# Attention and MLP block on one core: scores in bfloat16, and one exponential for some pairs of tiles

## The chip, the core and the metric

The kernel runs on one core of a Trainium2 chip. Its engines work side by side, each through its own queue in order: TensorE (PE in the profile, PEld for its weight loads), VectorE (DVE), ScalarE (ACT), GpSimd (POOL) and SyncE (SP), which here only issues DMAs. Engines wait for each other through semaphores. The metric is the device time in microseconds (us) of one execution; lower is better.

## The reference

A transformer block over 2048 tokens of width 640 with a modulation computed from a vector `c`. First attention with 32 heads of 128 against caches of 2048 keys and values, then a token-mixing MLP. The part that matters here is the attention:

```python
sa, ca, ga, sb, cb, gb = ...            # six rows from silu(c) @ w_mod
h = _layernorm(x) * (1 + ca) + sa
q = (h @ wq).reshape(B, Sq, H, Dh).transpose(0, 2, 1, 3)
scores = einsum('bhqd,bhkd->bhqk', q, k_cache) * Dh ** (-0.5)
p = softmax(scores)
o = einsum('bhqk,bhkd->bhqd', p, v_cache)
x = x + ga * (o.transpose(...).reshape(B, Sq, H * Dh) @ wo)
h = _layernorm(x) * (1 + cb) + sb
x = x + gb * B(h)                       # layernorm, w1, gelu, shifts, w2, then w3, gelu, w4
```

All inputs and the output are bfloat16.

## The kernel before

Work is written as a list of operations for each engine (class `Prog`); each names the keys it reads and writes, and the class derives the semaphore waits. An engine carries out its operations in the order in which they were written. An operation that reads what an earlier one of the same engine wrote waits for that one too, on DVE, ACT and GpSimd.

The attention stage is one loop over `s` (line 553), 512 tiles of 128 queries: head `h = s // 16`, tile `j = s % 16`. Step `s` does the following.

- PE computes the scores of the tile, 128x2048, into the PSUM tensor `Sps` in two halves of 1024 (`qk`, lines 301 and 15). Between the halves it multiplies the probabilities of the tile eight steps back, `g_ = s - PVD` with `PVD = 8`, by V (`pv`, line 314, 16 matrix products into `PTp`), and does pieces of other work: a query projection for the next head (`q_piece`, line 246), or a transposition on PE (`t_piece`, line 262).
- DVE reads each half of the scores from PSUM, multiplies by minus the scale, writes the result as fp32 to a ring of three slots, `negS[:, s % 3]`, and keeps the minimum of the half in `nm0` or `nm1` (line 594). The profile shows the write of the minimum as a separate instruction.
- GpSimd takes the smaller of the two minima (line 604), and ACT computes `exp(nm - negS)` over 128x2048 into the ring of probabilities `Pb`, ten slots (line 607). The per-partition `nm` is the bias operand.
- The probabilities have to be transposed for the product with V. For most tiles SP issues a DMA transpose, of two tiles at once where both of an even and odd pair go by DMA (`transpose`, line 231). Two tiles a head (3 and 10), three in every fourth head (2, 3 and 10), are transposed by PE instead, in two halves of 1024 columns, and each half is copied from PSUM by ACT (line 271); for tiles 2 and 3 DVE copies the second half (line 273, `by_dve`).
- On odd steps ACT copies the attention output of two tiles from PSUM to `Of` (line 585), and it copies finished query chunks to `QT` (line 253).
- Four steps later (`LAG`) GpSimd normalizes: for each group of four tiles one reciprocal of the row sums (`rcp`, line 455), a multiplication for each tile (`norm`, line 462) and, after the fourth, a store to a scratch in HBM, issued from GpSimd's own DMA queue (line 469).
- SP also issues the loads of K (line 214, a DMA transpose), wq and V for the following heads, in the same queue as the transposes.

PSUM holds only one tile of scores, so PE writes the next half as soon as DVE has read it, and PE, DVE, GpSimd, ACT, SP and DMA form a loop: the product with V for tile `s - 8` stands in PE's queue among the scores of tile `s`.

After the loop follow the output projection, the layernorms and the MLP, in which neither `Sps` scores nor exponentials occur; `negS` is reused there as storage.

Of the kernel before, what the change touches and what calls it, by code (L numbers as in the profile page):

```python
# [7 lines left out]
ACT = mybir.ActivationFunctionType  # L8
BF16 = mybir.dt.bfloat16
F32 = mybir.dt.float32  # L10
# [113 lines left out]
def bass_adaLN_cond__mha_block_cached__mixer_s_mlp__prompt_kernel(  # L124
# [3 lines left out]
    _, H, SK, DH = A_k_cache.shape  # L128
# [3 lines left out]
    NQT = SQ // 128  # L132
# [13 lines left out]
    with ExitStack() as es:  # L146
# [11 lines left out]
        if True:  # L158
            with ExitStack() as es1:
                sb1 = lambda name, shape, dt: es1.enter_context(nc.sbuf_tensor(name, shape, dt))  # L160
                RP = 10
                PVD = 8
                PE_STEPS = ({3: 6, 10: 13}, {2: 5, 3: 7, 10: 14})
                kind = lambda h: 1 if h % 4 == 1 else 0
                US = KT * (SQ + 4)
                sb1("pad", [128, 32], F32)
                ring = sb1("ring", [128, 2 * RP, SK], BF16)
                negS = sb1("negS", [128, 3, SK], F32)
                wo = sb1("wo", [128, H, D], BF16)
                kv = sb1("kv", [128, 2 * SK + 2 * NKT * 130 + 2 * KT * 128 + 2 * SQ], BF16)  # L170
                small = sb1("small", [128, 4 * NQT + 32], F32)
                hTx = sb1("hTx", [128, US], BF16)
                Of = sb1("Of", [128, 4, 2, 130], F32)
                On = sb1("On", [128, 2, 4, 128], BF16)
# [1 line left out]
                sd = small[:, 2 * NQT:3 * NQT]  # L176
                rstd = small[:, 3 * NQT:4 * NQT]
                nm0, nm1, nm, rl = [small[:, 4 * NQT + 8 * i:4 * NQT + 8 * i + 8] for i in range(4)]
                hT = hTx[:, 0:KT * SQ].rearrange("p (k q) -> p k q", k=KT)
                o1 = 2 * SK  # L180
                o2 = o1 + 2 * NKT * 130
# [5 lines left out]
                Pb = ring[:, 0:RP]  # L187
# [22 lines left out]
                G = Prog(nc, es1, "a")  # L210
# [61 lines left out]
                    else:  # L272
                        G.op("vector", lambda v: v.tensor_copy(dst, src), r=[("J", jb)], w=[("PT", g % RP, r)])  # L273

                by_dve = lambda g, r: r == 1 and g % NQT in (2, 3)
                PIECES = []
                for steps in PE_STEPS:
                    taken = [u for j in steps.values() for u in range(2 * j, 2 * j + 4)]
# [68 lines left out]
                if H > 1:  # L347
# [8 lines left out]
                     r=["id0"], w=["ident"])  # L356
# [122 lines left out]
                tmp = flat[:, 0:4 * D].bitcast(F32).rearrange("p (b d) -> p b d", b=2)  # L479
                xt = flat[:, XT0:XT0 + NQT * D].rearrange("p (t d) -> p t d", t=NQT)  # L480
                xb = flat[:, XB0:XB0 + 2 * NQT * D].bitcast(F32).rearrange("p (t d) -> p t d", t=NQT)
                negb = negS[:].rearrange("p r s -> p (r s)").bitcast(BF16)
                gT = [flat[:, GT0:GT0 + NFT4].rearrange("p (f q) -> p f q", f=NFT),
                      negb[:, 0:NFT4].rearrange("p (f q) -> p f q", f=NFT)]
                OTj = [hTx[:, 0:2 * H * 128].rearrange("p (h q) -> p h q", q=128),
# [15 lines left out]
                rst = sm[:, 288:288 + 3 * NQT].rearrange("p (l t) -> p l t", l=3)  # L501
                vet = sm[:, 336:336 + 3 * NQT].rearrange("p (l t) -> p l t", l=3)
                mhalf = sm[:, 384:385]
                NEG = [("negS", i) for i in range(3)]
                KVK = ([("KT", b) for b in range(2)] + [("V", b) for b in range(2)] + [("wq", b) for b in range(2)]
                       + [("QT", b, cc) for b in range(2) for cc in range(NQC)])
                HTK = [("hT", cc, k) for cc in range(NQC) for k in range(KT)]
# [43 lines left out]
                LAG = 4  # L551
                for s in range(NG + PVD + LAG):
                    h, j = divmod(s, NQT)
                    g_ = s - PVD
                    evacs = []
                    if s <= 2:
                        for i in ((0,), (1, 2), range(3, len(MROW)))[s]:
                            mod_rows(i)
                    if s == 3:
                        G.op("gpsimd", lambda g: g.tensor_scalar(  # L560
                            out=mod_bc[:, 2 * D:3 * D], in0=mod_bc[:, 2 * D:3 * D], scalar1=1.0, scalar2=1.0, op0=ALU.add, op1=ALU.mult),
                            r=[("mod", i) for i in range(len(MROW))], w=["mod"])
                    for half in range(2):
                        if s < NG:
                            qk(s, half)
                        if half == 0 and s in (NG + PVD - 5, NG + PVD - 4):
                            b0 = a_pe(0, None if s == NG + PVD - 5 else b0, (s - NG - PVD + 5,))
                        if half == 0 and s == NG + PVD - 2:
                            b1 = a_pe(1, None, (0,))
                        if 0 <= g_ < NG:  # L570
                            pv(g_, half)
                        if s == 0 and half == 1:
                            q_head0(NQC - 1)
                        if h + 1 < H and 2 * j + half in PIECES[kind(h)]:
# [13 lines left out]
                    for fn, x, y in evacs:  # L588
                        if fn is q_evac or not by_dve(x, y):
                            fn(x, y)  # L590
                    for half in range(2):
                        if s < NG:
                            r8 = s % 8
                            G.op("vector", lambda v, half=half, s=s, r8=r8: v.tensor_scalar(  # L594
                                out=negS[:, s % 3, half * 1024:(half + 1) * 1024],
                                in0=Sps[:, half * 1024:(half + 1) * 1024],
                                scalar1=-SCALE, scalar2=None, op0=ALU.mult, op1=ALU.min,
                                accum_out=(nm0 if half == 0 else nm1)[:, r8:r8 + 1]),
                                r=[("S", half)], w=[("negS", s % 3), ("nmh", half, r8)])
                    for fn, x, y in evacs:  # L600
                        if fn is t_evac and by_dve(x, y):
                            fn(x, y)
                    if s < NG:
                        G.op("gpsimd", lambda g, r8=r8: g.tensor_scalar(  # L604
                            out=nm[:, r8:r8 + 1], in0=nm0[:, r8:r8 + 1], scalar1=nm1[:, r8:r8 + 1], scalar2=None, op0=ALU.min),
                            r=[("nmh", 0, r8), ("nmh", 1, r8)], w=[("nm", r8)])
                        G.op("scalar", lambda a, s=s, r8=r8: a.activation(  # L607
                            Pb[:, s % RP, :], negS[:, s % 3, :], ACT.Exp, bias=nm[:, r8:r8 + 1], scale=-1.0),
                            r=[("negS", s % 3), ("nm", r8)], w=[("Pb", s % RP)])
                        if not is_pe(s):  # L610
                            if s % 2 == 1 and not is_pe(s - 1):
                                transpose(s - 1, 2)
                            elif s % 2 == 1 or is_pe(s + 1):
                                transpose(s, 1)
                        if j == 2 and h >= 1 and h + 1 < H:
                            load_k(h + 1)
                        if h + 1 == H and j in (2, PVD + 1):
                            i = 0 if j == 2 else 1
                            load_ot(0, OTC[i], OTC[i + 1], i)
                        if j == 6 and h + 2 < H:  # L620
                            load_wq(h + 2)
# [72 lines left out]
                for n in range(KT):  # L694
                    lst = []
                    p = 0
                    while p < 128:
# [8 lines left out]
                        p = pe_  # L706
# [203 lines left out]
```

## Time and profile before

| | |
|---|---|
| runs, median (3 runs) | 1574.97 us (1573.75 to 1576.16) |
| profiled execution: span from first to last instruction | 1568.9 us |
| first score instruction of DVE | 35.4 us |
| last score instruction of DVE ends | 1251.8 us |
| granted TensorE clock, mean | 0.998 |
| moved by DMA over the span | 334.59 MB |

The page gives for the profiled execution the span only; the runs' times include what lies around it. A line of the groups has the source line, the engine, the operation, what is written and read with shapes and types, the count, then the busy time in us and the mean of one in ns, and then the idle time of the engine just before them with what ended it. A line of the timeline has the start in us from the span's start, the time taken, the engine and the group; in square brackets stands the idle time before it. "SPq" is SP's queue of DMA issues. A line of waits has who waited, for whom, us in total, how many times, and the longest. The stage of interest lies between 35 and 1252 us, 32 heads one after the other.

### The profile page before, as it was taken

Reading aid. Unit: us, or ns where it says so; the run is one execution under the profiler, and the core shown is the slowest. Engines: PE = TensorE matmul, PEld = TensorE weight load, DVE = VectorE, ACT = ScalarE, POOL = GpSimd, SP = SyncE. Lnnn points to the kernel's source line nnn. Section 1 sums busy time; section 2 is a strip of 40 time slices with the busy share of each in tenths; the row PEclk is TensorE's granted clock in tenths of the full one; section 3 lists DMA queues with packets and bytes.
Section 4 is the critical chain, followed back from the end, with each engine's and each line's share of the span. In section 5 each row is a group of like instructions: output and inputs, shape, how many; then the busy total and the mean of one; then the engine's idle time right before and its main releaser. Section 6 shows DMA issues by size and latency. Waiting matters only on the chain.

```text
span 1568.9 us, 33553 instructions
## 1 busy us (share of the span) xinstructions
PE 1472.3 (94%) x13947; PEld 923.4 (59%) x13175; DVE 1398.3 (89%) x2471; ACT 1275.9 (81%) x1121; POOL 623.0 (40%) x1396
## 2 busy tenths in 40 slices
PE   5899999999999999999999999999999899999999
PEld 3466666666665566566656666566566655554545
DVE  6999999999999999999999999999999937667435
ACT  4999999999999999999999999999999900034230
POOL 0144444444444444444444444444444433323100
PEclk9999999999999999999999999999999999999999
DMA  9999999999999999999999999999999999725100
GB/s 298 239 221 239 237 242 237 233 241 243 237 240 233 239 232 232 240 236 235 229 237 236 233 243 249 226 242 243 235 241 237 238 246 190 157 53 144 38 22 34
DMA packets 1172828, 334.59 MB, mean 213 GB/s; under 512 B 1153280, under 2 KB 1166656, under 8 KB 1172672
## 3 DMA queue, kind: packets, MB, share of 16 engines
q1 hardware_dynamic: 1164192, 311.30, 100.8%
q0 software_dynamic: 6144, 16.79, 3.5%
q10 hardware_dynamic: 2336, 4.34, 0.8%
q8 instruction: 108, 1.77, 0.5%
q14 instruction: 48, 0.39, 0.1%
HBM read 43.48 MB, written 19.40 MB: 40 GB/s over the span
## 4 chain that ended last, share of the span: by engine, by line
ACT 40%; DVE 23%; PE 19%; DMA 9%; issue 7%; POOL 1%; POOLq 0%; DVEq 0%
ACT ring L607 32%; DVE negS L594 20%; DMA ring<-ring 8%; PE Sps L540 8%; PE Sps L847 4%; ACT ring L271 3%; ACT kv L253 2%; ACT Of L585 2%; PE QPp L798 2%; PE Oaug L798 2%; DVE ring L273 1%; PE Sps L783 1%; DVE ring L379 1%; DMA negS<-o_scratch 1%; PE PTp L314 1%
## 5 line engine op out<-in xcount | busy, mean ns | idle before, releaser
L594 DVE TENSOR_SCALAR_CACHE_REDUCE negS<-Sps 128x1024 f32<-128x1024 f32 x1024 | 1177.7, 1224 | 19.4 <-PE Sps L15 18.5
L607 ACT ACTIVATE ring<-negS,small 128x2048 bf16<-128x2048 f32 x512 | 1045.7, 2066 | 13.7 <-POOL small L604 12.5
L314 PEld LDWEIGHTS PTp<-kv,ring 128*128 128x128 bf16 x8192 | 554.1, 98 | 325.0 <-issue 69.6
L314 PE MATMUL PTp<-kv,ring 128*128 128x129 bf16 x8192 | 645.3, 220 | 25.0 <-DMA ring<-ring 23.9
L15 PE MATMUL Sps<-kv 128*128 128x512 bf16 x1024 | 387.9, 379 | 16.8 <-DVE negS L594 9.9
L604 POOL TENSOR_SCALAR small<-small 128x1 f32<-128x1 f32 x512 | 146.4, 286 | 621.8 <-DVE negS L594 621.7
L301 PE MATMUL Sps<-kv 128*128 128x512 bf16 x919 | 354.3, 386 | 27.8 <-DVE negS L594 16.5
L462 POOL TENSOR_SCALAR On<-Of,small 128x128 bf16<-128x128 f32 x512 | 191.0, 373 | 13.0
L301 PEld LDWEIGHTS Sps<-kv 128*128 128x128 bf16 x1024 | 98.1, 96 | 141.7 <-DVE negS L594 121.6
L455 POOL TENSOR_TENSOR small<-Of,small 128x4 f32<-128x4 f32 x128 | 133.1, 1040 | 8.8 <-ACT Of L585 8.7
L469 POOL DMA_DIRECT2D o_scratch<-On x128 | 103.1, 806 | 40.8 <-POOL On L462 37.2
L585 ACT COPY Of<-PTp 128x259 f32<-128x259 f32 x256 | 108.6, 424 | 13.2 <-PE PTp L314 13.2
L246 PE MATMUL Oaug<-hTx,kv 128*128 128x512 bf16 x268 | 101.9, 385 | 3.7 <-DVE hTx L411 3.7
L246 PE MATMUL QPp<-hTx,kv 128*128 128x512 bf16 x259 | 97.7, 382 | 2.6 <-ACT hTx L406 2.1
L728 ACT ACT_TABLE_LOAD x1 | 1.3, 1283 | 112.6 <-POOL hTx L746 112.6
L594 DVE DVE_READ_ACCUMULATOR negS<-Sps 128x1 f32 x1024 | 90.3, 88 | 0.0
L271 ACT COPY ring<-Oaug 128x1024 bf16<-128x1024 bf16 x72 | 77.0, 1069 | 0.0
L641 POOL TENSOR_SCALAR negS<-negS 128x1 f32<-128x1 f32 x48 | 24.2, 504 | 125.2 <-DVE negS L650 125.2
L540 PE MATMUL Sps<-wo,negS 128*128 128x128 bf16 (+1 forms) x503 | 69.9, 298 | 1.2 <-DMA negS<-o_scratch 0.8
L540 PE MATMUL Sps<-wo,hTx 128*128 128x512 bf16 (+1 forms) x502 | 69.3, 297 | 0.5
L851 DVE TENSOR_TENSOR ring<-Sps,ring 128x640 f32<-128x640 f32 x15 | 12.4, 824 | 59.5 <-PE Sps L847 59.5
L655 DVE TENSOR_TENSOR ring<-Sps,mod_bc 128x640 f32<-128x640 f32 x16 | 13.1, 821 | 53.6 <-PE Sps L540 32.9
(88 smaller groups left out, 1052.7 us busy)
## 6 DMA issues: line engine op xcount, KB each, us to landing
kv<-in_A_v_cache_dram SPq DMA_DIRECT2D x32, 512.0 KB, 5.0
o_scratch<-On POOLq DMA_DIRECT2D x128, 128.0 KB, 4.7
kv<-in_A_wq_dram SPq DMA_DIRECT2D x32, 160.0 KB, 3.2
wo<-in_A_wo_dram SPq DMA_DIRECT2D x1, 5120.0 KB, 16.5
ring<-ring SPq DMA_TRANSPOSE x248, 7.1
ring<-in_A_x_dram SPq DMA_DIRECT2D x5, 640.0 KB, 6.6
ring<-in_w_mod_dram SPq DMA_DIRECT2D x1, 3200.0 KB, 13.8
out_dram<-wo SPq DMA_DIRECT2D x15, 160.0 KB, 1.8
```

What stands on the lines that cost most here:

```text
L15: return t.add_instruction(mybir.InstMatmult(name=t.bass.get_next_instruction_name(), ins=[t.lower_ap(rhs), t.lower_ap(lhsT)], outs=[t.low ...
L246: G.op("tensor", lambda t: t.matmul(JB[jb], wq[:, hb, q, :], hT[:, q, cc * 512:(cc + 1) * 512], start=(q == 0), stop=(q == KT - 1)), r=[(" ...
L271: G.op("scalar", lambda a: a.copy(dst, src), r=[("J", jb)], w=[("PT", g % RP, r)])
L301: ins = (t.matmul if c2 == 0 else partial(same_weights, t))(Sps[:, col:col + 512], QT[:, hb, j * 128:(j + 1) * 128], KTs[:, hb, col:col + ...
L314: ins = t.matmul(ob[:, 0:129], PTs[:, b, kt, :], Vaug[:, hb, kt, 0:129], start=(kt == 0), stop=(kt == NKT - 1))
L455: G.op("gpsimd", lambda g: g.tensor_tensor(out=rl[:, 4 * b:4 * b + 4], in0=Of[:].rearrange("p a z d -> p (a z) d")[:, 4 * b:4 * b + 4, 128 ...
L462: G.op("gpsimd", lambda g: g.tensor_scalar(out=On[:, b, z, :], in0=Of[:, 2 * b + z // 2, z % 2, 0:128], scalar1=rl[:, 4 * b + z:4 * b + z ...
L540: ins = t.matmul(YB[b][:, c0:c0 + cw], OTj[pr % 2][:, 2 * hh + z, :], wo[:, hh, c0:c0 + cw], start=(hh == 0), stop=(hh == H - 1))
L585: G.op("scalar", lambda a, p=p: a.copy(Of[:, p % 4].rearrange("p z d -> p (z d)")[:, 0:259], PO[:, (p % 2) * 512:(p % 2) * 512 + 259]), r= ...
L594: G.op("vector", lambda v, half=half, s=s, r8=r8: v.tensor_scalar(out=negS[:, s % 3, half * 1024:(half + 1) * 1024], in0=Sps[:, half * 102 ...
L604: G.op("gpsimd", lambda g, r8=r8: g.tensor_scalar(out=nm[:, r8:r8 + 1], in0=nm0[:, r8:r8 + 1], scalar1=nm1[:, r8:r8 + 1], scalar2=None, op ...
L607: G.op("scalar", lambda a, s=s, r8=r8: a.activation(Pb[:, s % RP, :], negS[:, s % 3, :], ACT.Exp, bias=nm[:, r8:r8 + 1], scale=-1.0), r=[( ...
```

## The change

The scores' ring `negS` becomes bfloat16 with six slots (`NR`) in the same space, and the two minima of a tile are kept as bfloat16. GpSimd first copies the first minimum to fp32 (`nmf`), since it serves as a per-partition operand, then takes the smaller one.

For the tiles 0, 1, 4, 5, 8, 9, 12 and 13 of each head (`MERGED`), GpSimd subtracts the minimum from the 128x2048 scores in place, and after the odd tile one exponential over both tiles, 128x4096 without a bias operand, takes the place of two. For the other tiles the exponential stays as it was. All transposed halves of PE's tiles are copied by ACT (`by_dve` is never true). The product with V stands nine steps behind the scores (`PVD = 9`); the issue of the V load, tied to `PVD`, moves by one step too.

```diff
-                PVD = 8
+                PVD = 9
+                NR = 6
+                MERGED = (0, 4, 8, 12)
+                merged = lambda s: (s % NQT) // 2 * 2 in MERGED
-                negS = sb1("negS", [128, 3, SK], F32)
+                negS = sb1("negS", [128, NR, SK], BF16)
+                nmh = [t.bitcast(BF16)[:, 0:8] for t in (nm0, nm1)]
+                nmf = small[:, 4 * NQT + 32:4 * NQT + 40]
...
-                by_dve = lambda g, r: r == 1 and g % NQT in (2, 3)
+                by_dve = lambda g, r: False
...
-                                out=negS[:, s % 3, half * 1024:(half + 1) * 1024],
+                                out=negS[:, s % NR, half * 1024:(half + 1) * 1024],
-                                accum_out=(nm0 if half == 0 else nm1)[:, r8:r8 + 1]),
+                                accum_out=nmh[half][:, r8:r8 + 1]),
...
+                        G.op("gpsimd", lambda g, r8=r8: g.tensor_copy(nmf[:, r8:r8 + 1], nmh[0][:, r8:r8 + 1]),
+                             r=[("nmh", 0, r8)], w=[("nmf", r8)])
                         G.op("gpsimd", lambda g, r8=r8: g.tensor_scalar(
-                            out=nm[:, r8:r8 + 1], in0=nm0[:, r8:r8 + 1], scalar1=nm1[:, r8:r8 + 1], scalar2=None, op0=ALU.min),
+                            out=nm[:, r8:r8 + 1], in0=nmh[1][:, r8:r8 + 1], scalar1=nmf[:, r8:r8 + 1], scalar2=None, op0=ALU.min),
+                        if merged(s):
+                            G.op("gpsimd", lambda g, s=s, r8=r8: g.tensor_scalar(
+                                out=negS[:, s % NR, :], in0=negS[:, s % NR, :], scalar1=nm[:, r8:r8 + 1], scalar2=1.0,
+                                op0=ALU.subtract, op1=ALU.mult),
+                                r=[("nm", r8)], w=[("negS", s % NR)])
+                            if s % 2 == 1:
+                                G.op("scalar", lambda a, s=s: a.activation(
+                                    ring[:, (s - 1) % RP:s % RP + 1].rearrange("p r s -> p (r s)"),
+                                    negS[:, (s - 1) % NR:s % NR + 1].rearrange("p r s -> p (r s)"), ACT.Exp, scale=-1.0),
+                                    r=[("negS", (s - 1) % NR), ("negS", s % NR)], w=[("Pb", (s - 1) % RP), ("Pb", s % RP)])
+                        else:
-                        G.op("scalar", lambda a, s=s, r8=r8: a.activation(
-                            Pb[:, s % RP, :], negS[:, s % 3, :], ACT.Exp, bias=nm[:, r8:r8 + 1], scale=-1.0),
-                            r=[("negS", s % 3), ("nm", r8)], w=[("Pb", s % RP)])
+                            G.op("scalar", lambda a, s=s, r8=r8: a.activation(
+                                Pb[:, s % RP, :], negS[:, s % NR, :], ACT.Exp, bias=nm[:, r8:r8 + 1], scale=-1.0),
+                                r=[("negS", s % NR), ("nm", r8)], w=[("Pb", s % RP)])
```

More of the change, by code (lines that the diff above doesn't have):

```diff
@@ L167, in bass_adaLN_cond__mha_block_cached__mixer_s_mlp__prompt_kernel @@
                 ring = sb1("ring", [128, 2 * RP, SK], BF16)
-                negS = sb1("negS", [128, 3, SK], F32)
+                negS = sb1("negS", [128, NR, SK], BF16)
                 wo = sb1("wo", [128, H, D], BF16)
                 kv = sb1("kv", [128, 2 * SK + 2 * NKT * 130 + 2 * KT * 128 + 2 * SQ], BF16)
-                small = sb1("small", [128, 4 * NQT + 32], F32)
+                small = sb1("small", [128, 4 * NQT + 40], F32)
                 hTx = sb1("hTx", [128, US], BF16)
@@ L481, in bass_adaLN_cond__mha_block_cached__mixer_s_mlp__prompt_kernel @@
                 xb = flat[:, XB0:XB0 + 2 * NQT * D].bitcast(F32).rearrange("p (t d) -> p t d", t=NQT)
-                negb = negS[:].rearrange("p r s -> p (r s)").bitcast(BF16)
+                negb = negS[:].rearrange("p r s -> p (r s)")
                 gT = [flat[:, GT0:GT0 + NFT4].rearrange("p (f q) -> p f q", f=NFT),
@@ L503, in bass_adaLN_cond__mha_block_cached__mixer_s_mlp__prompt_kernel @@
                 mhalf = sm[:, 384:385]
-                NEG = [("negS", i) for i in range(3)]
+                NEG = [("negS", i) for i in range(NR)]
                 KVK = ([("KT", b) for b in range(2)] + [("V", b) for b in range(2)] + [("wq", b) for b in range(2)]
@@ L594, in bass_adaLN_cond__mha_block_cached__mixer_s_mlp__prompt_kernel @@
                             G.op("vector", lambda v, half=half, s=s, r8=r8: v.tensor_scalar(
-                                out=negS[:, s % 3, half * 1024:(half + 1) * 1024],
+                                out=negS[:, s % NR, half * 1024:(half + 1) * 1024],
                                 in0=Sps[:, half * 1024:(half + 1) * 1024],
                                 scalar1=-SCALE, scalar2=None, op0=ALU.mult, op1=ALU.min,
-                                accum_out=(nm0 if half == 0 else nm1)[:, r8:r8 + 1]),
-                                r=[("S", half)], w=[("negS", s % 3), ("nmh", half, r8)])
+                                accum_out=nmh[half][:, r8:r8 + 1]),
+                                r=[("S", half)], w=[("negS", s % NR), ("nmh", half, r8)])
                     for fn, x, y in evacs:
@@ L603, in bass_adaLN_cond__mha_block_cached__mixer_s_mlp__prompt_kernel @@
                     if s < NG:
+                        G.op("gpsimd", lambda g, r8=r8: g.tensor_copy(nmf[:, r8:r8 + 1], nmh[0][:, r8:r8 + 1]),
+                             r=[("nmh", 0, r8)], w=[("nmf", r8)])
                         G.op("gpsimd", lambda g, r8=r8: g.tensor_scalar(
-                            out=nm[:, r8:r8 + 1], in0=nm0[:, r8:r8 + 1], scalar1=nm1[:, r8:r8 + 1], scalar2=None, op0=ALU.min),
-                            r=[("nmh", 0, r8), ("nmh", 1, r8)], w=[("nm", r8)])
-                        G.op("scalar", lambda a, s=s, r8=r8: a.activation(
-                            Pb[:, s % RP, :], negS[:, s % 3, :], ACT.Exp, bias=nm[:, r8:r8 + 1], scale=-1.0),
-                            r=[("negS", s % 3), ("nm", r8)], w=[("Pb", s % RP)])
+                            out=nm[:, r8:r8 + 1], in0=nmh[1][:, r8:r8 + 1], scalar1=nmf[:, r8:r8 + 1], scalar2=None, op0=ALU.min),
+                            r=[("nmf", r8), ("nmh", 1, r8)], w=[("nm", r8)])
+                        if merged(s):
[12 more added lines that the diff above has]
+                                r=[("negS", s % NR), ("nm", r8)], w=[("Pb", s % RP)])
                         if not is_pe(s):
```

## The prediction

> **What bounds the kernel now.** I read the page's shares first, then one stretch of the attention stage, the groups, the waits, and the order of work on GpSimd and on the DMA queue.
>
> ```profile
> PE 1472.3 (94%) x13947; PEld 923.4 (59%) x13175; DVE 1398.3 (89%) x2471; ACT 1275.9 (81%) x1121; POOL 623.0 (40%) x1396
> POOL 0144444444444444444444444444444433323100
> 600.00:800.00 200.00, 187.34 (x1927) 120.95 (x1794) 195.55 (x341) 197.50 (x165) 91.20 (x209) 1.00 1.21 234
> ```
> The third line is one stretch of the attention stage (columns: length, then busy time of PE, weight loads, DVE, ACT, POOL). DVE and ACT have 4.5 and 2.5 us of 200 left, PE 13 (its ends are modelled); only POOL has room, 54%.
>
> ```profile
> L594 DVE TENSOR_SCALAR_CACHE_REDUCE negS<-Sps 128x1024 f32<-128x1024 f32 x1024 | 1177.7, 1224 | 19.4 <-PE Sps L15 18.5
> L607 ACT ACTIVATE ring<-negS,small 128x2048 bf16<-128x2048 f32 x512 | 1045.7, 2066 | 13.7 <-POOL small L604 12.5
> L604 POOL TENSOR_SCALAR small<-small 128x1 f32<-128x1 f32 x512 | 146.4, 286 | 621.8 <-DVE negS L594 621.7
> L462 POOL TENSOR_SCALAR On<-Of,small 128x128 bf16<-128x128 f32 x512 | 191.0, 373 | 13.0
> L560 POOL TENSOR_SCALAR mod_bc<-mod_bc 128x640 f32<-128x640 f32 x1 | 0.7, 726 | 0.0
> PE PTp L314 <- DMA ring<-ring: 23.9, 37, 1.7
> ```
> Budgets per head (16 steps, one tile each) come from start-to-start times in the trace, since neighbours overlap. The first score instruction of head 1 starts at 77.0 us and that of head 31 at 1214.2: 37.9 us a head. **DVE**: 32 halves at 1.144 (scale with minimum, plus its accumulator read) and 3 heads of 4 with one, the fourth with two copies at 0.603: 37.4. **ACT**: 16 exponentials at 1.905, 8 copies of the attention output at 0.255, 4 query copies at 0.469, 3 or 4 transposed halves at 0.898: 37.09 or 37.99, mean 37.3. **SP's queue**, which issues the transposes:
>
> ```profile
> 603.08 21.38 SPq L231 DMA_TRANSPOSE ring<-ring  x5
> 624.50 2.26 SPq L214 DMA_TRANSPOSE kv<-in_A_k_cache_dram  x1
> 626.80 5.43 SPq L231 DMA_TRANSPOSE ring<-ring  x1
> 632.28 0.58 SPq L218 DMA_DIRECT2D kv<-in_A_wq_dram  x1
> 632.91 8.94 SPq L231 DMA_TRANSPOSE ring<-ring  x2
> 641.89 0.58 SPq L223 DMA_DIRECT2D kv<-in_A_v_cache_dram  x1
> ```
> It goes without a pause through a head: 34.3 us for eight transposes, with the K, wq and V loads and gaps 38.3 (35.7 in every fourth head, which has seven), mean 37.6. In those heads most transposed pairs land under 0.6 us before PE multiplies by them, and PE waits 24 us in all. So three resources of nearly equal load, 37.3 to 37.6, give 37.9, and the fourth, POOL, has half its time free.
>
> **The change, part by part.** *Scores in bfloat16.* DVE still reads 1024 fp32 elements from PSUM for each instruction; nothing in the trace shows that this instruction's output type matters, and with its input unchanged I take 1.144 as it is. Six slots in place of three let DVE run further ahead of ACT: worth up to the gap between 37.9 and the largest load, no more.
>
> *Transposed halves to ACT.* DVE loses 0.60 or 1.21 a head and falls to 36.6. ACT gains 0.90 or 1.80.
>
> *One exponential for a pair.* The copies of 259, 512 and 1024 elements (0.255, 0.469, 0.898) cost 0.84 ns per element, so 2048 more elements cost 1.72 instead of another 1.905: 3.62 if the fixed part stays, 3.47 if only the copies' remains. L406 with two per-partition operands takes 780 ns where L802, the same size with none, takes 597: about 0.09 for the bias that goes. I take 3.53. Per head four pairs save 4 x (3.81 - 3.53) = 1.1. With the moved copies ACT stands at 36.9 or 38.7, mean 37.3: no gain.
>
> *GpSimd.* This is the part that decides. Every step gets a second small operation, and eight steps of a head a subtraction over 128x2048. The order of the queue now:
>
> ```profile
> 703.03 0.28 POOL L604 TENSOR_SCALAR small<-small 128x1 f32<-128x1 f32 x1 [2.26 <-DVE negS L594]
> 703.28 0.37 POOL L462 TENSOR_SCALAR On<-Of,small 128x128 bf16<-128x128 f32 x1
> 703.95 0.81 POOL L469 DMA_DIRECT2D o_scratch<-On  x1 [0.29 <-POOL On L462]
> 705.34 0.28 POOL L604 TENSOR_SCALAR small<-small 128x1 f32<-128x1 f32 x1 [0.58 <-DVE negS L594]
> 705.59 1.04 POOL L455 TENSOR_TENSOR small<-Of,small 128x4 f32<-128x4 f32 x1
> 706.74 0.38 POOL L462 TENSOR_SCALAR On<-Of,small 128x128 bf16<-128x128 f32 x1
> ```
> Start to start, the minimum takes 0.25 and a normalization 0.345. Once in four steps a reciprocal adds 1.14: its 1.04 and 0.10 before the normalization, which waits for it on the same engine. Once in four the store adds 1.17 (0.67 to its start and at least 0.85 to the next instruction, less the 0.345). A head before: 16 x 0.595 + 4 x 2.31 = 18.8 us.
>
> After, an unmerged step has the copy of the first minimum (no such row; 0.18, the shortest L641, also one element with constants; between the 0.10 of a one-element memset and the 0.28 of L604), 0.10 of waiting for it, the minimum 0.25, the normalization 0.345: 0.88. A merged step has the minimum's full 0.28, 0.10 more of waiting, the subtraction S, 0.03 of overlap, and the normalization: 0.98 + S. A head: 8 x 0.88 + 8 x 0.98 + 4 x 2.31 + 8 S = 24.1 + 8 S.
>
> S is not in the trace. From L462 (128 elements, 373 ns) to L560 (640, 726) an element costs 0.69 ns, which gives S = 1.70; but L462 has a per-partition operand and L560 has none. Taking 0.10 off L462 for it (L604 at 0.28 against 0.18) gives 0.885 ns and 2.07. L641 and L560 have the same form: 0.85 ns, and with L604's 0.28 S = 2.02. The memsets L769 and L770 (320 and 640 elements, 366 and 632 ns) give 0.83. Two-byte data buys nothing in L352 against L353 (206 and 204 ns), so I exclude a halving. I take 2.0, by the pair of one form: POOL 40.1 us a head (37.7 at S = 1.70, 40.7 at 2.07; the copy's bounds move it by -1.3 to +1.6).
>
> The Trainium skill, "GPSIMD Engine Reference", section 3.1, puts a one-input body of at most two operations at 1.03 cycles of 1.2 GHz for each element; an estimate by it is 1.76 plus L604's 0.28, so S = 2.04 and 40.4 us a head, which speaks for the upper rows and against the 1.70.
>
> That load is above every other, so POOL sets the pace if nothing starves it. In a merged pair it has 2 x (0.98 + 2.0) + 2.31 = 8.3 us to do in 5.0, in the next pair 1.8, so it ends the second subtraction some 4.5 us after DVE ended that tile. Queued behind the subtractions are the normalizations, the store and the minima that the next plain exponentials wait for; PE waits for none directly, but for the transposes behind the exponential: 4.5 + 3.5 + 7.2 (issue to landing of a pair) = 15.2 us. PE comes to the pair's first tile, now nine steps on, about 6.85 steps after DVE ended the second (that is where PE stands now with eight, 13.5 us, plus a step): 17.1 at 2.5 us a step. So 1.9 us remain, POOL stays fed, DVE, ACT and SP idle, and their small gains and losses lie hidden under it.
>
> **Sum.** 31 periods x (40.1 - 37.9) = 68; head 0 (41.6 now, with start-up work) some 0.5; at the end ACT has up to a merged exponential and a plain one in front of the last, 3 us more lag; the added step of PE at the end lies under the landing of the last transposes. 1568.9 + 72 = 1641 for the profiled span. The median of the runs stands 6.1 above the span: **1647 us**, its own range 1610 to 1690 from the bounds of S and of the copy.
>
> **Rivals.** *B, GpSimd keeps up* (the other side). If S is at most about 1.68, or the 0.10 waits vanish (24 a head, 2.4 us), POOL is at 37.6 or less and SP's 37.6 and ACT's 37.3 set the pace again, with looser buffers: 37.4 to 37.6, so 31 x 0.4 = 12 us less, 3 back at the end: 1566. For it: the raw slope of 0.69. Against: three rows at 0.83 to 0.885. Between the two lies no change, at S = 1.73.
> *C, the landings decide.* If the DMA queue still holds a pair back 2.5 us, as it does now in three heads of four, the way is 17.7 us in 6.85 steps, 2.58 a step, 41.3 a head: 31 x 3.4 + 3 = 108, 1683. For it: the slack of under 0.6 us now. Against: at a longer period the queue, 37.6 a head, has gaps and catches up. It decides from a delay of 1.9 us.
> *D, GpSimd and DVE get in each other's way.* In the last stage L641, one element, takes 0.18, 0.45 or 0.71 us, and over 0.8 at times. In the attention stage all 512 of L604 lie between 0.28 and 0.30 beside DVE's PSUM reads, so I see none there. If each subtraction grew by 0.5 us, 4 us a head: 1770.
>
> **How the numbers follow.** A 0.60, C 0.18, D 0.03, B 0.19, of which 0.14 come out faster by over 0.2% and 0.05 within it (0.2%, 3 us, is about what the spread of these runs can tell from no change). Slower: 0.81. The range leaves out B's faster part and the top: 1571 to 1700.
>
> **What would show it.** Right: POOL over 95% busy in the attention slices, its subtraction near 2.0 us and hardly any waiting for DVE in L604's successor; ACT's idle time before the exponentials ended by POOL; DVE waiting for free score slots or PE; PE's wait for transposes small; period near 40. Wrong: a subtraction of 1.7 or less, POOL waiting for DVE every step, ACT still at 99%. C shows as PE waiting long for the transposes while POOL has gaps. Each exponential of a pair should take about 3.6, score instructions 1.22.

## The result, and the profile after

The changed kernel takes 3139.09 us (median of 4 runs, 3137.79 to 3139.19), the kernel before in the same session 1575.57: a ratio of 1.994, 95% interval 1.991 to 1.998. The forecast was slower, at 1647 us in a range of 1571 to 1700; the direction is right, the size is not.

The page of the changed kernel, shares and two rows of its 40 slices:

```profile
PE 1752.4 (56%) x14199; PEld 1048.4 (33%) x13175; DVE 1403.2 (45%) x2431; ACT 1285.2 (41%) x1033; POOL 2551.7 (81%) x2164
...
POOL 4988899898998898998889888999888988893320
PEclk8777777677677776777777777777777777779999
```

GpSimd went from 40% to 81% of a span twice as long; DVE and ACT have nearly as many busy microseconds as before (1398 and 1276), over twice the time. The clock granted to TensorE is six or seven tenths in the slices in which GpSimd is 80% busy or more. Line numbers are those of each run's own kernel. In the changed one DVE's score instruction is L599, GpSimd's small copy L609, its minimum L611 and its subtraction L615. On ACT the merged exponential is L620, the plain one L625, the copy of the attention output L590 and that of a transposed half L276. On PE the product with V is L319, the query projection L251 and the transposition L267. The groups and the longest waits of the same page and trace:

```profile
L599 DVE TENSOR_SCALAR_CACHE_REDUCE negS<-Sps 128x1024 bf16<-128x1024 f32 x1024 | 1200.0, 1222 | 1569.4 <-PE Sps L15 1563.9
L615 POOL TENSOR_SCALAR negS<-negS,small 128x2048 bf16<-128x2048 bf16 x256 | 1841.5, 7193 | 23.9
...
L620 ACT ACTIVATE ring<-negS 128x4096 bf16<-128x4096 bf16 x128 | 462.9, 3616 | 1563.3 <-POOL negS L615 1563.3
L625 ACT ACTIVATE ring<-negS,small 128x2048 bf16<-128x2048 bf16 x256 | 505.3, 2008 | 0.0
...
L609 POOL CAST small<-small 128x1 f32<-128x1 bf16 x512 | 98.4, 192 | 8.7 <-DVE negS L599 7.5
```

```profile
DVE negS L599 <- PE Sps L15: 1563.9, 325, 14.0
ACT ring L620 <- POOL negS L615: 1563.3, 128, 15.0
...
PE PTp L319 <- ACT Of L590: 850.4, 89, 11.8
PE Oaug L251 <- ACT ring L276: 373.5, 31, 12.7
```

The second line of the groups tells most of it: the subtraction takes 7.19 us, not 2.0, and hardly varies (7.17 to 7.21 over 256). ACT's merged exponential waits 1563 us in all for it, 12.2 each; PE waits for ACT, and DVE for PE, 1564 us: one wait passed on. GpSimd's queue in one cycle of four steps, from the timeline:

```profile
1501.52 7.18 POOL L615 TENSOR_SCALAR negS<-negS,small 128x2048 bf16<-128x2048 bf16 x1
1508.67 1.04 POOL L460 TENSOR_TENSOR small<-Of,small 128x4 f32<-128x4 f32 x1
1509.82 0.37 POOL L467 TENSOR_SCALAR On<-Of,small 128x128 bf16<-128x128 f32 x1
...
1512.56 7.21 POOL L615 TENSOR_SCALAR negS<-negS,small 128x2048 bf16<-128x2048 bf16 x1
1519.74 0.37 POOL L467 TENSOR_SCALAR On<-Of,small 128x128 bf16<-128x128 f32 x1
1520.41 0.82 POOL L474 DMA_DIRECT2D o_scratch<-On  x1 [0.29 <-POOL On L467]
...
1521.93 7.18 POOL L615 TENSOR_SCALAR negS<-negS,small 128x2048 bf16<-128x2048 bf16 x1
```

The same instruction of the cycle returns after 20.41 us: 81.6 a head. The period over heads 1 to 31 is 87.05 us against 37.91. Where the 1568.5 us more of the span went: 30 periods x 49.1 = 1474; head 0 35.8; the last head 44.8; the end of the kernel 13.9.

### The profile page after: what moved, and what is told of

The parts are those of the page before. It is cut to its first block, busy times and chain, and to the rows that moved or that the text cites. A ratio compares the mean times of both kernels' runs of the same rounds, so it can differ in the third digit from the quotient of the medians.

```text
span 3137.4 us, 34420 instructions
## 1 busy us (share of the span) xinstructions
PE 1752.4 (56%) x14199; PEld 1048.4 (33%) x13175; DVE 1403.2 (45%) x2431; ACT 1285.2 (41%) x1033; POOL 2551.7 (81%) x2164
## 4 chain that ended last, share of the span: by engine, by line
POOL 70%; PE 12%; ACT 7%; issue 7%; DVE 4%; DMA 0%; POOLq 0%; DVEq 0%
POOL negS L615 57%; ACT ring L620 5%; PE Sps L545 4%; POOL On L467 4%; POOL small L611 4%; DVE negS L599 3%; POOL small L460 3%; POOL small L609 2%; PE Sps L865 2%; ACT ring L276 1%; PE QPp L816 1%; PE Oaug L816 1%; PE Oaug L251 1%; PE Sps L15 1%; PE Sps L306 1%
## 5 line engine op out<-in xcount | busy, mean ns | idle before, releaser
L599 DVE TENSOR_SCALAR_CACHE_REDUCE negS<-Sps 128x1024 bf16<-128x1024 f32 x1024 | 1200.0, 1222 | 1569.4 <-PE Sps L15 1563.9
L615 POOL TENSOR_SCALAR negS<-negS,small 128x2048 bf16<-128x2048 bf16 x256 | 1841.5, 7193 | 23.9
L319 PE MATMUL PTp<-kv,ring 128*128 128x129 bf16 x8192 | 768.1, 247 | 850.4 <-ACT Of L590 850.4
L319 PEld LDWEIGHTS PTp<-kv,ring 128*128 128x128 bf16 x8192 | 664.9, 112 | 1364.9 <-issue 1281.5
L620 ACT ACTIVATE ring<-negS 128x4096 bf16<-128x4096 bf16 x128 | 462.9, 3616 | 1563.3 <-POOL negS L615 1563.3
L625 ACT ACTIVATE ring<-negS,small 128x2048 bf16<-128x2048 bf16 x256 | 505.3, 2008 | 0.0
L306 PE MATMUL Sps<-kv 128*128 128x512 bf16 x1024 | 456.2, 445 | 5.2 <-DVE negS L599 2.8
L15 PE MATMUL Sps<-kv 128*128 128x512 bf16 x1024 | 448.5, 438 | 0.0
L251 PE MATMUL Oaug<-hTx,kv 128*128 128x512 bf16 x320 | 151.2, 477 | 375.9 <-ACT ring L276 373.5
L611 POOL TENSOR_SCALAR small<-small 128x1 f32<-128x1 bf16 x512 | 149.5, 292 | 221.0 <-DVE negS L599 175.0
L251 PEld LDWEIGHTS Oaug<-hTx,kv 128*128 128x128 bf16 x320 | 36.8, 115 | 386.0 <-ACT ring L276 283.2
L474 POOL DMA_DIRECT2D o_scratch<-On x128 | 104.9, 820 | 40.7 <-POOL On L467 37.2
L251 PE MATMUL QPp<-hTx,kv 128*128 128x512 bf16 x320 | 124.1, 392 | 2.3 <-ACT hTx L411 1.6
L267 PE MATMUL QPp<-ident,ring 128*128 128x128 bf16 x576 | 62.3, 237 | 82.4 <-ACT ring L276 82.4
L609 POOL CAST small<-small 128x1 f32<-128x1 bf16 x512 | 98.4, 192 | 8.7 <-DVE negS L599 7.5
L267 PE MATMUL Oaug<-ident,ring 128*128 128x128 bf16 x576 | 74.5, 270 | 51.9 <-ACT ring L625 51.6
L590 ACT COPY Of<-PTp 128x259 f32<-128x259 f32 x256 | 93.1, 364 | 16.3 <-PE PTp L319 16.3
L599 DVE DVE_READ_ACCUMULATOR negS<-Sps 128x1 bf16 x1024 | 88.0, 86 | 0.0
```

Source lines behind the costliest of these rows:

```text
L15: return t.add_instruction(mybir.InstMatmult(name=t.bass.get_next_instruction_name(), ins=[t.lower_ap(rhs), t.lower_ap(lhsT)], outs=[t.low ...
L251: G.op("tensor", lambda t: t.matmul(JB[jb], wq[:, hb, q, :], hT[:, q, cc * 512:(cc + 1) * 512], start=(q == 0), stop=(q == KT - 1)), r=[(" ...
L306: ins = (t.matmul if c2 == 0 else partial(same_weights, t))(Sps[:, col:col + 512], QT[:, hb, j * 128:(j + 1) * 128], KTs[:, hb, col:col + ...
L319: ins = t.matmul(ob[:, 0:129], PTs[:, b, kt, :], Vaug[:, hb, kt, 0:129], start=(kt == 0), stop=(kt == NKT - 1))
L609: G.op("gpsimd", lambda g, r8=r8: g.tensor_copy(nmf[:, r8:r8 + 1], nmh[0][:, r8:r8 + 1]), r=[("nmh", 0, r8)], w=[("nmf", r8)])
L611: G.op("gpsimd", lambda g, r8=r8: g.tensor_scalar(out=nm[:, r8:r8 + 1], in0=nmh[1][:, r8:r8 + 1], scalar1=nmf[:, r8:r8 + 1], scalar2=None, ...
```

## The experiments

All ran beside the kernel before, whose medians were 1569 to 1574 us there. "Period" is the mean time per head from the first score instruction of head 1 to that of head 31.

| run | time, us | ratio to before (95%) | period |
|---|---|---|---|
| e2_no_merge | 1588.30 | 1.012 (1.009 to 1.015) | 38.48 |
| e4_act_copies | 1590.17 | 1.013 (1.011 to 1.016) | 38.51 |
| e7_rings | 1574.85 | 1.000 (0.998 to 1.001) | 37.89 |
| e3_two_pairs | 2520.19 | one run | 67.82 |
| e8_two_pairs_later | 2487.39 | one run | 66.72 |
| e5_add | 1876.23 | 1.192 (1.190 to 1.194) | 47.56 |
| e6_balanced | 1829.62 | 1.162 (1.161 to 1.164) | 45.94 |
| e9_one_later | 1632.21 | 1.040 (1.038 to 1.042) | 39.73 |
| e10_two_later | 1629.51 | 1.038 (1.036 to 1.040) | 39.71 |
| e11_add_two_later | 1684.00 | 1.073 (1.071 to 1.075) | 41.42 |
| e12_tiles_3_7 | 1630.92 | 1.035 (1.033 to 1.038) | 39.76 |

**What makes the subtraction slow** (e1_pool_forms). A kernel of GpSimd operations alone, three of each form:

```python
G.op("gpsimd", lambda g: g.tensor_scalar(out=yh[:, 0:2048], in0=xh[:, 0:2048], scalar1=p, scalar2=1.0, op0=S, op1=M))
...                                     # the other forms, with other operations, types and lengths
# S subtract, A add, M mult, MX min; p a per-partition operand; x, y input and output; f fp32, h bfloat16
```

> Leaves the whole block out; only GpSimd elementwise operations over 128xN run, one form after another, nothing beside them. Theory T1 (two-byte input is slow): every form with bfloat16 input takes about 7.2 us at 2048 elements (3.5 ns an element), every form with fp32 input about 1.9 to 2.1, whatever the operation and whether in place. T2 (the operation: subtract with a per-partition operand and a second operation is slow): fp32 forms of it take 7.2 too, and bfloat16 forms with constants or with a single operation about 2.0. T3 (in place): only the in-place forms take 7.2. T4 (contention in the attention stage with DVE, ACT or DMA): all forms take about 2.0 here, since nothing runs beside them. If none of these but the length matters, 128 to 1024 elements lie on a line of 0.7 to 0.9 ns an element and 2048 lies above it.

Groups of that run, by form (last number: mean of one in ns, then idle time):

```profile
L151 POOL TENSOR_SCALAR yf<-xf,sc 128x2048 f32<-128x2048 f32 x3 | 21.5, 7160 | 0.3
L155 POOL TENSOR_SCALAR xh<-xh,sc 128x2048 bf16<-128x2048 bf16 x3 | 21.5, 7160 | 0.2
L157 POOL TENSOR_SCALAR yh<-xh 128x2048 bf16<-128x2048 bf16 x3 | 21.3, 7085 | 0.2
L163 POOL TENSOR_SCALAR yf<-xf,sc 128x2048 f32<-128x2048 f32 x3 | 16.3, 5434 | 0.3
L172 POOL TENSOR_SCALAR yf<-xf,sc 128x1024 f32<-128x1024 f32 x3 | 11.1, 3703 | 0.3
L161 POOL TENSOR_SCALAR yh<-xh,sc 128x2048 bf16<-128x2048 bf16 x3 | 5.9, 1972 | 0.3
L160 POOL TENSOR_SCALAR yh<-xh 128x2048 bf16<-128x2048 bf16 x3 | 5.7, 1897 | 0.2
L174 POOL TENSOR_SCALAR yf<-xf 128x640 f32<-128x640 f32 x3 | 2.2, 724 | 0.2
L169 POOL TENSOR_SCALAR yf<-xf,sc 128x128 f32<-128x128 f32 x3 | 2.1, 716 | 0.2
```

L151 and L155 are subtract with a per-partition operand, fp32 to a second tile and bfloat16 in place: the same 7160 ns, so neither type nor place matters (T1 and T3 fall), nor what runs beside it (T4 falls; 7193 in the attention stage). L157 is subtract with constants: 75 ns less. L161 is multiply with the per-partition operand, L160 add with constants: 1972 and 1897. L163 is a single minimum: 5434. So it is the operation, as T2 has it, but not the per-partition operand, and not a second operation as such: add and multiply have one too. A subtraction without a second operation was not run. From 128 to 1024 and 2048 elements subtract costs 3.33 and 3.38 ns an element; add from 640 (L174) to 2048 0.83.

**What the rest of the change does** (e2, e4, e7).

```diff
-                MERGED = (0, 4, 8, 12)
+                MERGED = ()                                    # e2: the changed kernel; e7: and by_dve as before
...
-                by_dve = lambda g, r: r == 1 and g % NQT in (2, 3)
+                by_dve = lambda g, r: False                    # e4: the kernel before
```

> The changed kernel with no merged pair: bfloat16 scores in six slots, nine steps to the product with V, all transposed halves copied by ACT, two small GpSimd operations a step; no subtraction, every exponential with its bias. Theory (the subtraction alone makes the slowdown; without it the budgets per head decide): DVE 36.6, SP 37.6, ACT 38.0 or 39.8, mean 38.4, POOL 24; so ACT, 31 x 0.5 above the time before: about 1592 us. Rival (the deeper rings and the ninth step free more than ACT loses): 1562 or less. Rival (other parts of the change cost much too): 1700 and more.

> The kernel before with one edit: ACT copies all transposed halves. Theory (ACT is one of three loads of nearly equal size, so what it gains it pays): ACT 38.0 or 39.8 us a head, mean 38.4 against 37.3: 1590 to 1605 us. Rival (DMA transposes bound three heads of four, so only the fourth pays): about 8 x 1.9 = 15 us in all from those heads alone, 1575 to 1590. Rival (DVE was the bound, and loses 0.6 to 1.2 us a head): 1555.

> The changed kernel with no merged pair and with DVE copying its halves as in the kernel before: left of the change are bfloat16 scores in six slots, the ninth step, and the small copy on GpSimd. Theory (the waits between three nearly equal loads were worth 0.3 us a head, and deeper rings take them away): 37.6 a head, 1560 to 1566 against 1570. Rival (the rings were deep enough): 1569 to 1575, the same. Rival (the small copy or the ninth step costs): over 1576.

Without the merged pairs the change costs 1.2%, and the copies moved to ACT alone cost 1.3%. In both the period is 38.5, where ACT's budget said 38.4, and ACT has no idle time at all from the first scores of head 1 to those of head 31, while DVE has 1.5 us a head. So the first theory of each holds. The time alone would not tell in e4: 1590 us lies on the edge of its theory and of its first rival, but by that rival ACT would have had idle time in three heads of four. With DVE copying as before (e7), bfloat16 scores, six slots, the ninth step and the small copy together do nothing: 37.89 against 37.91. So deeper rings buy nothing that can be seen here, against the theory of e7: ACT stands idle 0.36 us a head with them and 0.35 before. The four parts were not run one by one.

**Addition in place of subtraction** (e5).

```diff
-   out=nm..., in0=nmh[1]..., scalar1=nmf..., scalar2=None, op0=ALU.min)
+   out=nm..., in0=nmh[1]..., scalar1=nmf..., scalar2=-1.0 if merged(s) else 1.0, op0=ALU.min, op1=ALU.mult)
...
-                                op0=ALU.subtract, op1=ALU.mult),
+                                op0=ALU.add, op1=ALU.mult),
```

> The changed kernel with one edit: the minimum of a merged tile is negated in the instruction that forms it, and the large operation adds it in place of subtracting. Theory (the duration of the subtraction was the only mis-sized term): the operation takes 1.97 us, GpSimd has 24.1 + 8 x 1.97 = 39.9 us a head and sets the pace, the time is 62 + 4 above the kernel before: 1635 to 1645. Rival (the budget's other terms were too large, or GpSimd keeps up): 1575 to 1600. Rival (the merged exponential, waiting for GpSimd, holds the copies behind it on ACT, and PE with them, so that the waits come on top of the load): 1660 and more.

The group of the operation, and PE's waits in the first 1500 us (from 80 on):

```profile
L616 POOL TENSOR_SCALAR negS<-negS,small 128x2048 bf16<-128x2048 bf16 x256 | 505.9, 1976 | 23.9
```

```profile
PE PTp L319 <- ACT Of L590: 103.1, 69, 3.5
PE Oaug L267 <- ACT ring L626: 84.2, 51, 1.8
PE Oaug L251 <- ACT ring L276: 54.5, 27, 3.5
```

The operation is 1.98 us, as expected, and saves 1263 us. But the period is 47.6 and not 39.9, and the second rival's shape is right: PE waits for ACT three ways. It waits for the copy of the attention output, which frees its PSUM bank; for probabilities that it transposes itself; and for the copy of a transposed half. These three and the smaller ones of the kind are 279 us of the 302 by which this run is above the kernel before. All three stand in ACT's queue behind a merged exponential that waits for GpSimd, 305 us in all.

**Fewer pairs, and one step in ACT's order** (e3, e8; both with the slow subtraction).

```diff
-                MERGED = (0, 4, 8, 12)
+                MERGED = (0, 8)                                # e3 and e8
...
+                    for fn in later:                           # e8: behind the step's copies on ACT
+                        fn()
+                    later = []
...
-                                G.op("scalar", ...)            # the merged exponential; its transpose follows
+                                later.append(both)             # both: the exponential and its transpose
```

> The changed kernel with two merged pairs a head (tiles 0, 1, 8, 9) in place of four. Theory (GpSimd's queue is the bound, and its load is the sum of its instructions, with the subtraction at 7.19 us): 14.1 + 9.2 + 4 x 7.29 = 52.5 us a head, with one wait of 4.4 us a head 56.9; so 2030 to 2165 us. Rival (each merged pair costs a stall of its own, a quarter of the added 49 us a head): 62.5 us a head, 2340 us.

> The kernel with two merged pairs and the slow subtraction, with one edit: the merged exponential and its transpose are issued one step later, behind that step's copy of the attention output on ACT. Theory (with two pairs the time above GpSimd's own load, 68 against 52.5 us a head, comes from the exponential that waits for GpSimd and keeps the copy behind it, for which PE waits): PE gets two tiles further before it stops, up to 4.6 us for each pair, 9 a head, about 2240 us against 2520. Rival (PE stops for the probabilities themselves, not for that copy): 2500 or more.

Both theories missed. With two pairs the period is 67.8, 15 above GpSimd's load and above the rival too. ACT and PE in e3, from its timeline:

```profile
1544.41 3.62 ACT L620 ACTIVATE ring<-negS 128x4096 bf16<-128x4096 bf16 x1 [14.39 <-POOL negS L615]
1547.93 0.35 ACT L590 COPY Of<-PTp 128x259 f32<-128x259 f32 x1
```

```profile
1548.43 1.03 PE L319 MATMUL PTp<-kv,ring 128*128 128x129 bf16 x8 [12.38 <-ACT Of L590]
```

For each pair ACT stands 14.4 us, PE is free again when the 0.35 us copy behind the exponential is done, and only then can DVE go on and give GpSimd the next tile: the two loads come after each other. Moving that copy ahead (e8) gave 1.1 us a head in place of 9, since PE then stopped at the next thing it needs from ACT:

```profile
PE Oaug L267 <- ACT ring L632: 495.1, 37, 14.6
```

This is its own transposition (L267), which needs a plain exponential that is queued behind the merged one. That is what the rival of e8 names, that PE stops for the probabilities themselves, and 2487 us is near its 2500. Each of the two times is of a single run.

**All exponentials later in the order** (e6, e9, e10, e11). e6 is e5 with fp32 minima and so without the small copy, and DVE copies the second half of tile 2. e9 and e10 are e6, and e11 is e5, with every exponential and its transpose one (e9) or two steps later. With them go the product with V, ten steps behind the scores, and in three heads of four PE's transpositions; in every fourth head these stay where they were. The normalization keeps its step:

```diff
-                by_dve = lambda g, r: False
+                by_dve = lambda g, r: r == 1 and g % NQT == 2          # e6, e9, e10
...
-                PVD = 9
+                PVD = 10
-                PE_STEPS = ({3: 6, 10: 13}, {2: 5, 3: 7, 10: 14})
+                PE_STEPS = ({3: 8, 10: 14}, {2: 5, 3: 7, 10: 14})      # e9: {3: 7, 10: 14} first
...
-                LAG = 4
+                LAG = 3
+                LATE = 2                                               # e9: 1
+                late = []
...
+                    while late and late[0][0] <= s:                    # after the step's copies
+                        late.pop(0)[1]()
...
+                        late.append((min(s + LATE, NG), exps))         # exps: exponential and transpose
```

> The kernel with the addition, minima kept as fp32 (so no small copy on GpSimd), and DVE still copying the second transposed half of tile 2 in every fourth head. Budgets per head: GpSimd 35.6, ACT 36.9 or 37.8, DVE 36.6 or 37.2, SP 37.6. Theory (the budgets per head add up and SP's queue is the largest): 37.6 a head, 1560 to 1568, just below the kernel before. Rival (with four pairs the waits of ACT for GpSimd, a lag of about 4 us behind DVE in each pair, come through to PE): 1590 to 1620.

> The balanced kernel (addition, fp32 minima), with every exponential and its transpose one step later in ACT's and SP's order, the product with V ten steps behind, and PE's transposition of tiles 3 and 10 one step later in three heads of four. Theory (PE stops because ACT, waiting for GpSimd, keeps copies and probabilities back that PE needs within two to three steps; the rings do not help against an order): one step is 2.3 of the lag of some 4 us, so half of the 8.4 us a head above 37.6 goes: near 41.5 a head, 1680 to 1720 against 1830. Rival (PE stops for the landing of the transposes or another resource): 1800 and more.

> The same with two steps and tile 3 transposed at step 8. Theory: 4.6 us cover the lag, the budgets per head decide again, SP 37.6 and ACT 36.9 or 37.8: 37.6 to 38.2 a head, 1560 to 1590. Rival (the way from score to product with V, now with exponentials two steps later, is too long for ten steps): PE waits for landing transposes, 1600 to 1700. Rival as above: 1800 and more.

> The changed kernel with the addition (bfloat16 minima, the small copy, all halves copied by ACT), with exponentials two steps later, as above. Theory (with the waits gone GpSimd's load of 39.9 us a head is the bound): 1635 to 1650 against 1876. Rival (GpSimd's load does not add up so, and ACT's 37.3 decides): 1560 to 1590. Rival (the waits stay): 1800 and more.

e6 shows that the small copy and ACT's load were not the main part: 45.9 a head with GpSimd at 35.6, only 1.6 less than in e5 and above both of its forecasts. A step of delay takes 197 us away (1829.6 to 1632.2), of the 256 by which e6 is above the kernel before, and the second step 3 more. Neither theory had the time: e9 gained more than it said, and e10 stayed above its 1590. The 1629.5 us of e10 lie in the range of its first rival, but PE waits only 20 us for landing transposes, which that rival names, and 60 for probabilities (below). The loads of the engines are the same in e6, e9 and e10, so it was the order and the distance of the work in the queues that made the waits, and not a load. How much of it was the exponentials' place on ACT, and how much PE's later steps, was not separated. In every fourth head, where PE's transpositions were not moved, the period only went from 43.3 to 42.4 us; in the other three it went from 46.8 to 38.8.

In e11, the changed kernel with the addition, 47.6 becomes 41.4 against GpSimd's 39.9; its 1684 us is above the 1650 of the theory. In the stretch of 600 to 800 us GpSimd is 173.9 us busy, and with its own waits, some 4.1 us a head by the budget, near 194 of 200. So its load is nearly the bound there, and the budget is right to 4%.

**What holds e10 above 37** (e12).

```diff
-                PE_STEPS = ({3: 8, 10: 14}, {2: 5, 3: 7, 10: 14})
-                kind = lambda h: 1 if h % 4 == 1 else 0
+                PE_STEPS = ({3: 10, 7: 14}, {3: 10, 7: 14})
+                kind = lambda h: 0
...
-                by_dve = lambda g, r: r == 1 and g % NQT == 2
+                by_dve = lambda g, r: False
```

> The balanced kernel with exponentials two steps later, with PE transposing tiles 3 and 7 in every head, at steps 10 and 14, in place of tiles 3 and 10 (2, 3 and 10 in every fourth head), and all halves copied by ACT. Theory (what is left in the kernel before this one above 37 us a head is PE standing at step 14 for the probabilities of tile 10, and at step 5 of every fourth head for tile 2, whose exponentials are then only two or one step old in ACT's order): these waits go, budgets per head are DVE 36.6, ACT 36.9, GpSimd 35.6, so 36.9 to 37.4 a head; the end of the kernel is 6 us longer with ten steps: 1545 to 1562 against 1569. Rival (SP's queue with eight transposes in every head, 38.3 a head, is now the bound): 1585 to 1590. Rival (PE waits for ACT elsewhere): 1600 to 1630.

Waits of e10, and then of e12, both from 80 to 1280 us:

```profile
PEld Oaug L267 <- ACT ring L625: 66.3, 36, 3.6
PE Oaug L267 <- ACT ring L625: 60.0, 36, 3.4
```

```profile
PEld PTp L319 <- DMA ring<-ring: 129.1, 94, 4.0
PE PTp L319 <- DMA ring<-ring: 76.0, 68, 3.3
```

The waits for ACT are gone, and the time is the same. PE now waits for the landing of transposes, most at step 10, where tile 0 of a merged pair is due (54 of the 76 us). Head by head e10 takes 42.8 us in every fourth head, where PE has three tiles, and 38.6 in the others; in e12, whose heads are all alike, the same two groups take 40.0 and 39.7. So the edit took away the long heads, as the theory had it, and made the others longer. No forecast holds: the time is just above the range of the last rival, but PE's waits for ACT, which it names, are nearly gone. The first rival names SP's queue, but at 38.3 a head it does not explain 39.8: in e12 the queue stands idle 2.4 us a head. How much comes of the queue and how much of the later issue of the pairs was not separated. No version here is faster than the kernel before.

## Why the prediction was wrong, point by point

**The direction and its first cause were right.** GpSimd's queue was named as the part that decides, and its sum 24.1 + 8 S holds: with S = 7.19 it gives 81.6 us a head, and the cycle of 20.41 us above is 81.6. The single items came out as priced: the small copy 0.19 (0.18), its wait 0.10 (0.10), the minimum's 0.28 to 0.30 (0.28).

**The step that failed is S.** It was taken as 2.0 us from rows that differ from the subtraction in size, type and operand; that they also differ in the operation was not weighed. L462 multiplies and L560 and L641 add. The trace before has no GpSimd subtraction at all, so its price was open, and the ends 1.70 and 2.07 were far too close; 7.19 was measured, 5.2 us more in each of eight subtractions a head. For add and multiply the reading was right (1.98 in e5, 1.97 in e1_pool_forms, 2.0 taken). The Trainium skill, "GPSIMD Engine Reference", section 3.1, with its 1.03 cycles for each element of a one-input body of at most two operations, agrees with add and multiply (0.83 ns an element in e1_pool_forms) and differs from subtract by four times and from a single minimum by three; the measurement decides.

**A second step failed, and only e5 could show it.** "PE waits for none directly, but for the transposes behind the exponential" was wrong, and with it the 1.9 us said to remain and the 1647 even at S = 2.0: that kernel takes 1876. The path counted was from score to transposed probabilities, nine steps long. The short ones were missed: ACT's own copies and the probabilities that PE transposes three steps on stand behind the waiting exponential. A list of what is queued behind a wait was made for GpSimd, and not for ACT.

**ACT, DVE and SP.** The merged exponential measured 3.62, 3.52 from start to start (3.53 taken). The score instruction is 1222 ns (1224 before). That ACT gains nothing in sum is borne out in part: without pairs the moved copies cost 0.6 us a head, where its budget said 0.5. A pair gives back 0.28 us on ACT, as priced (3.52 against twice 1.90), but no run shows it in its time, since something else held each of them. The gap between 37.9 and the largest load was the right bound for the deeper rings, and none of it was seen to close (e7). In the changed kernel "their small gains and losses lie hidden" held. SP's 37.6 was not a load like the others: the same transposes and loads kept its queue busy for 34.0 us a head in the changed kernel, where they had more room, against 37.2 before. And that most transposed pairs land under 0.6 us ahead of PE holds for two of the three kinds of head with eight transposes (0.4 and 0.5 in the median); in the heads right behind a fourth one it is 1.5.

**The remaining 5.4 us a head** between 81.6 and 87.05 are waits of GpSimd for DVE, mostly once a head at tile 8, 4.4 us each. The sign "over 95% busy" was so not met: GpSimd is busy 179 of 200 us in the stage. "POOL stays fed" was nearly right with the long subtraction and wrong with the short one, where the wait per pair weighs more against the load.

**The rivals.** C (the landings decide) does appear, but only in e12, once ACT's order and PE's tiles are out of the way. D was not it: what runs beside GpSimd lengthens the subtraction by 0.03 us at most (7160 ns alone, 7193 in the stage). B fell with S.

## What to carry to other kernels

In these runs the price of an elementwise operation on GpSimd went by its operation (1.97 us to add or multiply, 7.16 to subtract, over 128x2048 with a per-partition operand). A row of another operation is no bound for it, and adding a negated operand can cost about a quarter of subtracting. Where an instruction is made to wait, list what is queued behind it on its own engine and when others need that: here a wait that nine steps should have covered came through after two or three. Where several loads are within a few per cent of each other, taking one away shows the next: here changes of order moved the wait from ACT's copies to PE's tiles and then to the landings, and none went below the start.

## What the runs showed of the hardware

In e1_pool_forms a single minimum on GpSimd with a per-partition operand costs 5.43 us for 2048 elements, between add or multiply (1.90 to 1.97) and subtract (7.09 to 7.16), fp32 and bfloat16 alike; copies and casts of that size take 1.89.

The clock granted to TensorE was lower in the changed kernel, 0.767 against 0.998 in the mean. Behind one of PE's waits for ACT:

```profile
1514.00 0.63 PE L306 MATMUL Sps<-kv 128*128 128x512 bf16 x1
1514.42 0.63 PE L15 MATMUL Sps<-kv 128*128 128x512 bf16 x1
...
1519.21 0.38 PE L306 MATMUL Sps<-kv 128*128 128x512 bf16 x1
1519.42 0.38 PE L15 MATMUL Sps<-kv 128*128 128x512 bf16 x1
```

The two score products stand 0.42 us apart at first, and 0.21 five microseconds later. The Trainium skill, "TensorE: Matmul & The Clock Gate", Part 1, has the clock halved after an idle window of about 3.4 us and restored after a busy one; the trace agrees with the halving after a gap of 8.3 us and with a return within some 5 us. What it cost was not measured; outside the 5.4 us a head in which GpSimd waited for DVE, GpSimd set the pace.
